# Attention steps with little filler: the value products behind the third score, the fourth score and the maxima behind them

## The chip, the cores and the metric

One Trainium2 chip, of which the program uses one core. The metric is the device time of one execution in microseconds (us); for each kernel the median of several executions is taken.

A core has several engines that run side by side, each working through its own list of instructions in order. TensorE (in the profile PE, its weight loads PEld) multiplies matrices and writes the results to PSUM, a small memory of eight banks. VectorE (DVE) and ScalarE (ACT) read PSUM and compute. GpSimd (POOL) computes on ordinary on-chip memory, and SyncE (SP) issues most of the transfers. An instruction that needs another engine's result waits on a semaphore, and everything behind it on the same engine waits too.

## The reference

Two attention layers and two gated feed-forward layers, interleaved, over 2048 tokens of width 448. The attention has 16 query heads of width 28 that share one key head and one value head. All weights are used twice, once in each layer.

```python
def _A_ref(x, wq, wk, wv, wo):            # S = 2048, D = 448, H = 16, Dh = 28
    q = (x @ wq).reshape(B, S, H, Dh).transpose(0, 2, 1, 3)
    k, v = x @ wk, x @ wv
    p = softmax(einsum("bhqd,bkd->bhqk", q, k) * Dh ** -0.5)
    o = einsum("bhqk,bkd->bhqd", p, v)
    return o.transpose(0, 2, 1, 3).reshape(B, S, H * Dh) @ wo

def _B_ref(x, w_gate, w_up, w_down):      # F = 1792
    return (sigmoid(x @ w_gate) * (x @ w_up)) @ w_down

x = x + _A_ref(layernorm(x)); x = x + _B_ref(layernorm(x))
x = x + _A_ref(layernorm(x)); x = x + _B_ref(layernorm(x))
```

## The kernel before

**Steps.** The attention of a layer is a loop of 256 steps (line 922): 16 units of queries (`u`, 128 tokens with all 16 heads each) times 16 tiles of keys (`kt`, 128 tokens each). One step does four kinds of work.

- **S, the scores** (`scores`, line 507). Four TensorE products of one key tile with four heads of the unit's queries each, 512 columns (line 510). Each goes to a PSUM bank of its own; ScalarE takes its exponential (line 513) and writes a tile `P` in ordinary memory, which sets the bank free.
- **P, the products with the values** (`pv`, line 516). They use the four tiles `P` of the step *before*, so they never wait for this step's exponentials. In the profile they are eight matmuls a step (each of the four fp32 products is run as two), and they add up in a bank of their own, not one of those that the scores use. Behind the last key tile of a unit the same function has ScalarE copy the sum out (line 525).
- **M, the maxima for the next unit** (`mx_gen`, line 464). Four more TensorE products (line 480), 512 columns each, for which VectorE takes the maximum over the keys (line 484). The scores of the next unit are shifted by these maxima. One such group of four is done per step; in two steps of a layer (`MORE`, line 902) there are two groups.
- **X, the side work** (lines 935 to 947). `tick` moves one finished unit at a time through its stages: sums, the output projection (12 matmuls, line 612), the layer norm, the split into halves, transfers. In layer 0, `paced` also lets the preparation of the weights go on, ScalarE's squares of 24 weight pieces among it (line 109).

**Filler.** Between these, at each letter F of the order, `fill.slice` (line 767) puts in matmuls of other stages, so that TensorE has work while ScalarE and VectorE drain the banks. The fillers are the query projections (`qp`, line 345 by way of `qproj`) and the feed-forward of finished blocks (`gp`, `up`, `dn`). Each matmul has a planned cost in nanoseconds (216 for one of 512 columns, 190 for one of 448, 110 for one of 256). `rate` is the planned filler of a step: what is left, divided by the steps until the next block can be fed (line 945). Each F gets a quarter of it, and what goes over is a debt on later slices. Side work, such as the output projection, counts against the same account.

**The order of a step** is one string, and the program issues the letters in this order on every engine:

```python
ORDER = "FSFSFSFSPXM"
```

So on TensorE a step is: filler, score 1, filler, score 2, filler, score 3, filler, score 4, value products, side work, maxima.

**Banks.** Scores, maxima and fillers share seven PSUM banks (line 45). A tile gets a bank that is free or next to become free in the plan of the compiler's tile layer, and its first matmul waits until the last reader of that bank is done. A query projection keeps a bank over all of its 11 matmuls, which at a low rate takes several steps; then six are left for the eight tiles of a step, four scores and four maxima.

**What is done with little filler.** At the start of a layer only the remaining query projections are there as filler, and the first feed-forward block comes in at step 49 (`FIRST`, line 903: 16 × 2 + 16 = 48 steps). From then on each block brings a planned 49,840 ns for 32 steps.

Of the kernel before, what the change touches and what calls it, by code (L numbers as in the profile page):

```python
# [19 lines left out]
def interleaved_layers_kernel(ctx: ExitStack, tc: tile.TileContext, x, wq, wk, wv, wo, wg, wu, wd, out, layers=2):  # L20
# [8 lines left out]
    F = wg.shape[1]  # L29
# [40 lines left out]
    def flush(every=False):  # L70
        todo, pend[:] = pend[:], []
        for i, (due, fn) in enumerate(todo):
            if due > now[0] and not every:
                pend.append((due, fn))
            else:
                fn()
        if every and pend:
            flush(True)
# [198 lines left out]
    def paced(step):  # L277

        k = next((i for i in range(len(PLAN) - 1) if PLAN[i + 1][0] > step), None)
        if k is None:  # L280
            n = 10 ** 6
        else:
            (a, p), (b, q) = PLAN[k], PLAN[k + 1]
            n = p + (q - p) * (step + 1 - a) / (b - a)
        while prepd[0] < n and ready[0] < 2 + FC:
            next(prep[0])
            prepd[0] += 1
# [70 lines left out]
    def layer_tiles(l):  # L358
        KK[l] = lay.tile([128, 2, S], F16, tag="KK", name="KK")
        VV[l] = lay.tile([128, KT, 32], F32, tag="VV", name="VV")  # L360
        nc.vector.memset(VV[l][:, :, 28:32], 0.0)
        nc.vector.memset(VV[l][:, :, 28:29], 1.0)
# [58 lines left out]
    def qgen(l, b):  # L421

        XT = XTQ.pop((l, b))
        for g in range(G):
            yield from qproj(l, XT, b, g)
        flush(True)
# [32 lines left out]
    def mx_ready(l, n):  # L459

        u, r = divmod(n, 4 * NB)
        return KVD[l] >= 4 * (r // 4 + 1) if u == 0 else True
# [44 lines left out]
    def scores(l, u, kt, g, P):  # L507
        assert ("m", l, u) in stored, (l, u, kt)
        s = psf.tile([128, 512], F32, tag=BANKS["s"], name="s", bufs=NBK[BANKS["s"]])
        nc.tensor.matmul(s, KK[l][0:96, 0, kt * 128:(kt + 1) * 128], QS[l, u][:, g].rearrange("p h n -> p (h n)"),  # L510
                         start=True, stop=True)
        p = wk1.tile([128, 512], F32, tag="P", name="P", bufs=8)
        nc.scalar.activation(p, s, AF.Exp, scale=esc)  # L513
        P.append(p)

    def pv(l, u, kt, P):
        if kt == 0:
            PVS[l, u] = psv.tile([128, 512], F32, tag="v", name="pv")
        v = PVS[l, u]
        for g in range(4):  # L520
            nc.tensor.matmul(v[32 * g:32 * g + 32], VV[l][:, kt], P[g], start=kt == 0, stop=kt == KT - 1,  # L521
                             tile_position=(0, 32 * g))
        if kt == KT - 1:
            o = wk1.tile([128, 512], F32, name="pvs", bufs=1)
            nc.scalar.copy(o, v)
            PVS[l, u] = o
# [5 lines left out]
    def later(*stages):  # L532

        side.append([stages[0][0], list(stages)])

    def tick():

        for s in list(side):
            s[0] -= 1
            if s[0] <= 0:  # L540
                flush()
                fill.run(s[1].pop(0)[1]())
                if s[1]:
                    s[0] = s[1][0][0]
                else:
                    side.remove(s)
# [235 lines left out]
    fill = Filler()  # L782
# [115 lines left out]
        nmx += 1  # L898

    early[0] = False  # L900
    ORDER = "FSFSFSFSPXM"
    MORE = (5, 10)
    FIRST = KT * TB + 16
    KEEP = 28000
# [1 line left out]
    for l in range(layers):  # L906
        mx = mxs[l]
        final = l + 1 == layers
        if not final:
            layer_tiles(l + 1)  # L910
        if l:
            for b in range(2, NB):
                fill.add(qgen(l, b), G * QCH)
        fill.slice(QCH)
        flush(True)
        next(mx, None)
        while late:
            late.pop(0)[1]()
        fill.slice(QCH)
        prevP = None  # L920
        rate = 0.0
        for step in range(U * KT):
            u, kt = divmod(step, KT)
            P = []
            for o in ORDER:
                if o == "S":
                    scores(l, u, kt, len(P), P)
                elif o == "M":
                    for _ in range(1 + (u == 0 and kt in MORE)):
                        next(mx, None)  # L930
                elif o == "P":
                    if prevP is not None:
                        pv(*prevP)
                elif o == "X":
                    if u and kt == 1:
                        b = (u - 1) // TB
                        if (l, b) not in BLK:
                            BLK[l, b] = Block(l, b)
                        later(*BLK[l, b].tile(u - 1))
                    if l == 0:  # L940
                        paced(step)
                    tick()
                    fed = sum(BLK[l, b].fed == TB for b in range(NBL) if (l, b) in BLK)
                    if fed < NBL - 1:
                        rate = fill.left / max(FIRST + TB * KT * fed - step, 1)
                    else:
                        rate = max(fill.left - KEEP, 0) / (U * KT - step)
                else:
                    fill.slice(rate / ORDER.count("F"))
            prevP = (l, u, kt, P)  # L950
        pv(*prevP)
        flush(True)
        later(*BLK[l, NBL - 1].tile(U - 1))
        if not final:
            mxs[l + 1] = mx_gen(l + 1)
        n = done = 0
        while (side or pend or fill.gens) if final else (side or pend or done < 4 * NB):
            tick()
            for _ in range(4):
                fill.slice(VS / 4)  # L960
            n += 1
            if not final and done < 4 * NB and QDONE.get((l + 1, 0)) == G and mx_ready(l + 1, done):
                if n >= 5 or done >= 4 * (NB - 1):
                    next(mxs[l + 1])
                    done += 1
                    n = 0
# [21 lines left out]
```

## Time and profile before

| what | value |
|---|---|
| median of 3 runs | 2358.69 us (2357.77 to 2359.82) |
| the profiled execution's own time | 2358.22 us |
| its span, first to last instruction | 2356.4 us |
| mean granted TensorE clock | 0.985 |
| TensorE busy | 2239.1 us, 95% of the span |
| VectorE busy | 1635.5 us, 69% |
| ScalarE busy | 1559.2 us, 66% |
| scores (line 510) | 2048 matmuls, 381 ns each |
| value products (line 521) | 4096 matmuls, 607 ns each, overlapping: 547.3 us together |
| maxima (line 480) | 2048 matmuls, 392 ns each, overlapping: 223.2 us together |
| exponentials (line 513) | 2048, 690 ns each |
| reductions for the maxima (line 484) | 2048, 681 ns each |

How to read it. A row of the timeline gives the start in us, the duration, the engine, the line, the operation, the tiles, and how many instructions of one kind are merged in the row. In brackets stands for how long the engine was idle before it, and which engine's instruction ended that idle time. TensorE's matmuls are pipelined and their ends are modelled, so the durations of neighbours overlap, and "busy" is no measure of what it could do: what counts is the distance from one start to the next. The share of busy time is a mean over stages that have different limits, so a change to some steps is read from those steps.

### The profile page before, as it was taken

The numbers are of one execution on the slowest core, as the hardware profiler recorded it, in microseconds if no ns is written. First come the engines' busy times: TensorE is split into PE (matmuls) and PEld (weight loads), VectorE is DVE, ScalarE is ACT, GpSimd is POOL, SyncE is SP. The second block draws the span as 40 slices with busy tenths as digits, with TensorE's granted clock in tenths as the row PEclk, the third lists the DMA queues.
The fourth block names the chain that finished last, engine by engine and source line by source line (L and its number), as shares of the span: only waits on it lengthen the run. The fifth ranks groups of instructions, "written<-read, shape, count | busy, mean of one in ns | idle before, by whom it ended". The sixth has DMA issues, their size and how long they took to land.

```text
span 2356.4 us, 41206 instructions
## 1 busy us (share of the span) xinstructions
PE 2239.1 (95%) x15736; PEld 1003.2 (43%) x15736; DVE 1635.5 (69%) x2917; ACT 1559.2 (66%) x2598; POOL 336.8 (14%) x602
## 2 busy tenths in 40 slices
PE   5888899999999999999998989999999999999999
PEld 3322243444444444444572224444444444444456
DVE  6888787777777777773358877867676777777321
ACT  5588676776667677677413777767676776767751
POOL 5203763100110110001101011000000000000010
PEclk9799999999999999999998999999999999999999
DMA  3244652323313132333342112222231313223133
GB/s 114 65 126 124 201 190 81 90 73 98 96 58 109 58 93 70 94 92 78 96 139 53 27 49 92 87 78 83 62 103 58 98 55 101 76 82 94 57 111 119
DMA packets 208071, 213.88 MB, mean 91 GB/s; under 512 B 139952, under 2 KB 168304, under 8 KB 207872
## 3 DMA queue, kind: packets, MB, share of 16 engines
q1 hardware_dynamic: 202496, 196.36, 28.5%
q0 software_dynamic: 5376, 14.87, 1.8%
q8 instruction: 123, 2.02, 0.4%
q14 instruction: 76, 0.62, 0.1%
HBM read 175.37 MB, written 23.59 MB: 84 GB/s over the span
## 4 chain that ended last, share of the span: by engine, by line
PE 51%; DVE 5%; DMA 1%; ACT 1%; issue 0%; SPq 0%; POOL 0%; ACTq 0%; DVEq 0%; POOLq 0%
PE pv L521 12%; PE s L510 10%; PE dn L702 8%; PE gp L345 7%; PE up L345 7%; DVE mp L484 4%; PE mx L480 4%; PE wo L612 2%; PE qp L345 1%; ACT P L513 0%; DMA sums<-rc 0%; DMA KK<-ktl 0%; DMA rc<-sums 0%; DMA sums<-pvs 0%; DVE st L297 0%
## 5 line engine op out<-in xcount | busy, mean ns | idle before, releaser
L513 ACT ACTIVATE P<-s,esc 128x512 f32<-128x512 f32 x2048 | 1307.8, 690 | 509.2 <-PE s L510 492.1
L484 DVE TENSOR_REDUCE mp<-mx 128x1 f32<-128x512 f32 x2048 | 1267.2, 681 | 412.2 <-PE mx L480 408.1
L510 PE MATMUL s<-QS,KK 96*128 96x512 f16 x2048 | 761.1, 381 | 52.7 <-DVE mp L484 34.8
L345 PEld LDWEIGHTS <-wgu 128*128 128x128 f16 x4928 | 458.6, 98 | 241.3 <-issue 94.5
L521 PE MATMUL pv<-P,VV 128*32 128x512 f32 x4096 | 547.3, 607 | 0.0
L345 PE MATMUL up<-XT,wgu 128*128 128x256 f16 x2464 | 375.6, 272 | 0.8 <-DVE mp L484 0.8
L345 PE MATMUL gp<-XT,wgu 128*128 128x256 f16 x2464 | 375.2, 274 | 0.2
L702 PE MATMUL dn<-WD,h 128*128 128x448 f16 x1344 | 321.7, 352 | 0.0
L510 PEld LDWEIGHTS <-KK 96*128 96x128 f16 x2048 | 194.5, 97 | 172.1 <-issue 93.0
L480 PE MATMUL mx<-KK,QH 32*128 32x512 f16 x2048 | 223.2, 392 | 20.7 <-ACT QH L402 4.8
L480 PEld LDWEIGHTS <-QH 32*128 32x128 f16 x2048 | 53.5, 91 | 396.5 <-issue 378.1
L702 PEld LDWEIGHTS <-h 128*128 128x128 f16 x1344 | 124.1, 98 | 136.6 <-issue 22.6
L521 PEld LDWEIGHTS pv<-P,VV 128*32 128x32 f32 x4096 | 80.9, 108 | 204.4 <-issue 192.6
L595 POOL TENSOR_TENSOR lb<-pvs,lb 128x512 f32<-128x512 f32 x32 | 40.5, 1265 | 800.3 <-DMA lb<-sums 679.4
L676 ACT ACTIVATE h<-th 128x512 f16<-128x512 f32 x112 | 70.2, 627 | 86.4 <-DVE th L673 86.3
L345 PE MATMUL qp<-XT,WQ 128*128 128x512 f16 x352 | 114.5, 403 | 3.8 <-DVE mp L484 2.4
L673 DVE SCALAR_TENSOR_TENSOR th<-th,up 128x512 f32<-128x512 f32 x112 | 75.8, 677 | 59.0 <-PE up L345 46.5
L303 POOL TENSOR_SCALAR rs<-mv 128x1 f32<-128x1 f32 (+2 forms) x53 | 13.6, 256 | 686.4 <-DVE mv L298 682.9
L677 DVE SCALAR_TENSOR_TENSOR h<-th,h 128x512 f16<-128x512 f32 x112 | 77.7, 693 | 46.7 <-ACT h L676 46.7
L665 ACT ACTIVATE th<-gp,gsc 128x512 f32<-128x512 f32 x112 | 76.8, 685 | 47.7 <-PE gp L345 47.7
L612 PE MATMUL wo<-WO,oT 128*128 128x448 f16 x384 | 78.4, 353 | 0.3 <-DVE oT L602 0.2
L345 PEld LDWEIGHTS <-WQ 128*128 128x128 f16 x352 | 34.2, 101 | 64.2 <-issue 41.1
(126 smaller groups left out, 834.3 us busy)
## 6 DMA issues: line engine op xcount, KB each, us to landing
wgu<-wgu_d SPq DMA_DIRECT2D x224, 512.0 KB
QS<-qd SPq DMA_DIRECT2D x384, 32.0 KB
lb<-sums SPq DMA_DIRECT2D x128, 64.0 KB
xr<-in_A_x_dram SPq DMA_DIRECT2D x32, 224.0 KB
qd<-qst POOLq DMA_DIRECT2D x28, 256.0 KB, 2.7
wgu_d<-sgu POOLq DMA_DIRECT2D x14, 512.0 KB, 3.8
QH<-qd SPq DMA_DIRECT2D x28, 128.0 KB
x2d<-x SPq DMA_DIRECT2D x16, 224.0 KB
```

What stands on the lines that cost most here:

```text
L345: nc.tensor.matmul(ps, a, b, start=n == 0, stop=n == 10)
L480: nc.tensor.matmul(ps[h], qh[32 * h:32 * h + 32, g], KK[l][32 * h:32 * h + 32, 1, kb * 512:(kb + 1) * 512], start=True, stop=True, tile_po ...
L484: nc.vector.tensor_reduce(mp[:, g, h, kb:kb + 1], ps[h], axis=AX.X, op=OP.max)
L510: nc.tensor.matmul(s, KK[l][0:96, 0, kt * 128:(kt + 1) * 128], QS[l, u][:, g].rearrange("p h n -> p (h n)"), start=True, stop=True)
L513: nc.scalar.activation(p, s, AF.Exp, scale=esc)
L521: nc.tensor.matmul(v[32 * g:32 * g + 32], VV[l][:, kt], P[g], start=kt == 0, stop=kt == KT - 1, tile_position=(0, 32 * g))
L612: nc.tensor.matmul(p, v["oT"][:, a, h * 128:(h + 1) * 128], WO[:, c, h], start=n == 0, stop=n == 11)
L665: defer(lambda: nc.scalar.activation(th, gp.rearrange("p j n -> p (j n)"), AF.Tanh, scale=gsc))
L673: nc.vector.scalar_tensor_tensor(t, th, 1.0, up.rearrange("p j n -> p (j n)"), op0=OP.add, op1=OP.mult)
L676: nc.scalar.activation(h[:, 0], t, AF.Copy, scale=2.0 ** -17)
L677: defer(lambda: nc.vector.scalar_tensor_tensor(h[:, 1], t, 2.0 ** -17, h[:, 0], op0=OP.mult, op1=OP.subtract), 1)
L702: nc.tensor.matmul(p, hs[f // 2][:, a, o:o + 128], WD[:, f, c], start=n == 0, stop=n == 3 * FC - 1)
```

## The change

```diff
@@ -898,7 +898,8 @@
     early[0] = False
-    ORDER = "FSFSFSFSPXM"
+    FULL, POOR = "FSFSFSFSPXM", "FSFSFSPFSXM"
+    ENOUGH = 800
     MORE = (5, 10)
@@ -922,7 +923,8 @@
             u, kt = divmod(step, KT)
             P = []
-            for o in ORDER:
+            order = FULL if rate > ENOUGH else POOR
+            for o in order:
                 if o == "S":
                     scores(l, u, kt, len(P), P)
@@ -946,7 +948,7 @@
                 else:
-                    fill.slice(rate / ORDER.count("F"))
+                    fill.slice(rate / order.count("F"))
             prevP = (l, u, kt, P)
```

A step whose planned filler, as the step before has left it in `rate`, is at most 800 ns takes the order `POOR`; the others keep the old one. Both strings have the same letters: four F, four S, one each of P, X and M. In `POOR` the value products stand behind the third score. The fourth slice of filler and the fourth score follow them, then the side work and the maxima. So the value products are moved past one slice of filler and one score, and nothing is added or left out.

## The prediction

> **What bounds the kernel now.** The page comes first, for the span and for where TensorE (PE) is not dense.
>
> ```profile
> span 2356.4 us, 41206 instructions
> PE 2239.1 (95%) x15736; PEld 1003.2 (43%) x15736; DVE 1635.5 (69%) x2917; ACT 1559.2 (66%) x2598; POOL 336.8 (14%) x602
> PE   5888899999999999999998989999999999999999
> DVE  6888787777777777773358877867676777777321
> ```
>
> Over most of the span PE is at 9 tenths; at the start of each layer (slices 2 to 5 and 22 to 24) it falls to 8, and there DVE rises to 8. The change acts there. The rate at step 1 is the projections left over by the 48 steps before a block is fed: stepping the planner's account of matmul costs through the program gives 417 ns in layer 0 and 297 in layer 1. It stays under 800 through step 44 of layer 0 and step 45 of layer 1; then the last leftovers are divided by two or three steps, and from step 49 a block brings over 1,500 a step. As the order goes by the rate that the step before left, 45 + 46 = 91 of the 512 steps change. The second view sums the engines over these steps, without the first of each layer, which has no value products: layer 1 (45 steps), layer 0 (steps 1 to 28, then 29 to 44), and last a stretch of dense steps.
>
> ```profile
> 1273.66:1423.84 150.18, 135.12 (x809) 33.94 (x808) 125.95 (x216) 114.05 (x190) 12.87 (x25) 1.00 0.14 41
> 102.26:200.88 98.62, 88.23 (x517) 22.69 (x516) 78.99 (x133) 89.45 (x167) 7.46 (x14) 0.98 0.42 120
> 200.88:262.32 61.44, 51.83 (x303) 13.58 (x300) 50.27 (x93) 45.10 (x75) 34.97 (x34) 0.97 0.51 154
> ...
> 1475.00:1534.00 59.00, 58.88 (x444) 28.36 (x443) 45.42 (x79) 44.33 (x71) 4.63 (x10) 1.00 0.29 87
> ```
>
> After the stretch come its length and the busy time of PE, PEld, DVE, ACT and POOL, then the granted clock. In layer 1 nothing is full: DVE is busy for 126 of 150 us, ACT for 114. In steps 1 to 28 of layer 0 ACT is busy for 89 of 98.6 us. In the dense steps PE is busy for 58.9 of 59. So layer 1 must be held by a loop of waits, which one step of the timeline shows.
>
> ```profile
> 1339.09 0.39 PE L480 MATMUL mx<-KK,QH 32*128 32x512 f16 x4
> 1339.41 0.39 PE L510 MATMUL s<-QS,KK 96*128 96x512 f16 x1
> 1339.51 2.48 DVE L484 TENSOR_REDUCE mp<-mx 128x1 f32<-128x512 f32 x4 [0.58 <-PE mx L480]
> 1339.64 0.38 PE L345 MATMUL qp<-XT,WQ 128*128 128x512 f16 x1
> 1339.86 0.77 PE L510 MATMUL s<-QS,KK 96*128 96x512 f16 x2
> 1339.90 2.42 ACT L513 ACTIVATE P<-s,esc 128x512 f32<-128x512 f32 x4 [0.71 <-PE s L510]
> 1340.85 0.38 PE L510 MATMUL s<-QS,KK 96*128 96x512 f16 x1 [0.22 <-DVE mp L484]
> 1341.16 1.06 PE L521 MATMUL pv<-P,VV 128*32 128x512 f32 x8
> 1342.15 0.39 PE L480 MATMUL mx<-KK,QH 32*128 32x512 f16 x4
> 1342.58 2.48 DVE L484 TENSOR_REDUCE mp<-mx 128x1 f32<-128x512 f32 x4 [0.58 <-PE mx L480]
> ```
>
> Count from the first reduction, at 1339.51; a reduction in the row of four takes 2.48 / 4 = 0.62. The third score is the last of its row, 0.38 before its end: 1340.25, or +0.74, 0.1 behind the end of the first reduction. The fourth waits for the second (1.24 + 0.1 = +1.34): a projection holds one of the seven banks, so the eight tiles of a step share six. Behind the fourth score stand the value products (+1.65) and the maxima (+2.64), which DVE needs 0.43 later: +3.07. DVE, idle for 0.58, starts over. The loop is second reduction, fourth score, value products, maxima, first reduction.
>
> **The change, part by part.** It removes and adds no instruction. In 89 of the 91 steps (the first step of a layer has no value products) the eight value matmuls move on PE past one score and one slice of filler; no transfer moves with them, on SP's queue or POOL's. Let T3 and T4 be the starts of the third and the fourth score. Before, the maxima start at the later of T4 and T3 + 0.22 (the spacing of two scores), plus 0.31 to the value products, plus 0.99 to the maxima. After, the value products follow the third score, so the wait of the fourth passes under them, but two more changes of operand lie on the way: score to value products, and fourth score to maxima.
>
> ```profile
> 1271.32 1.03 PE L510 MATMUL s<-QS,KK 96*128 96x512 f16 x4
> 1272.28 0.57 PE L480 MATMUL mx<-KK,QH 32*128 32x512 f16 x3
> ...
> 1354.08 1.06 PE L521 MATMUL pv<-P,VV 128*32 128x512 f32 x8
> 1355.07 2.44 PE L612 MATMUL wo<-WO,oT 128*128 128x448 f16 x12
> ```
>
> Four scores in 1.03 are (1.03 - 0.38) / 3 = 0.22 apart, so the last starts at 1271.97, and the maxima behind it at +0.31. Behind value products a full-height matmul starts after 0.99, as the maxima do. No row shows a score there; the nearest is this 0.99, and its bounds are 0.99 and 0.99 + 0.10 (the weights not hidden, below). After: T3 + 0.31 + 0.99 + 0.31 = T3 + 1.61, if no filler falls in the fourth slice. A step thus gains max(0.22, T4 - T3) - 0.31: in the step above 0.60 - 0.31 = **0.29**, leaving 2.78 and DVE still idle for 0.30. In a step without a wait it loses 0.09.
>
> The fourth slice of filler costs too. Before, its matmul lay under the wait of the fourth score; after, it stands between value products and fourth score and adds 0.22. With a wait the gain shrinks to 0.07; where the filler alone made the distance, as here (1292.27 - 1291.84 = 0.43), the step loses 0.10.
>
> ```profile
> 1291.84 0.38 PE L510 MATMUL s<-QS,KK 96*128 96x512 f16 x1 [0.24 <-ACT P L513]
> 1292.05 0.38 PE L345 MATMUL qp<-XT,WQ 128*128 128x512 f16 x1
> 1292.27 0.38 PE L510 MATMUL s<-QS,KK 96*128 96x512 f16 x1
> ...
> 1277.76 0.38 PE L510 MATMUL s<-QS,KK 96*128 96x512 f16 x1 [0.16 <-DVE mp L484]
> ...
> 1417.96 0.82 PE L510 MATMUL s<-QS,KK 96*128 96x512 f16 x2 [0.56 <-ACT P L513]
> ```
>
> Reading T4 - T3 off all 45 steps of layer 1: 24 wait without filler there (the last two rows are the fourth score of the first of these, and third and fourth of the last), 0.53 apart on average, so 24 x 0.22 = 5.3; 9 wait with filler, 0.64 apart, 9 x 0.11 = 1.0; 12 don't wait, -12 x 0.09 = -1.1. Layer 1: **5.2**. In layer 0 the same reading of steps 29 to 44 gives **1.1**, without step 40, whose fourth score waits 3.3 us on ACT in either order. The waits themselves bound this:
>
> ```profile
> DVE mp L484 <- PE mx L480: 22.6, 33, 3.2
> PE s L510 <- DVE mp L484: 7.5, 31, 0.5
> PE s L510 <- ACT P L513: 2.7, 6, 0.6
> ...
> L109 ACT ACTIVATE rmax<-rmax 128x784 f32<-128x784 f32 x24 | 22.3, 928 | 0.0
> L109 ACT ACTIVATION_READ_ACCUMULATOR rmax<-rmax 128x1 f32 x24 | 6.5, 273 | 0.0
> ...
> L402 ACT ACTIVATE qst<-qp 128x512 f16<-128x512 f32 x5 | 3.0, 610 | 0.0
> ```
>
> The first three rows are those of layer 1's stretch: PE waited for scores' banks 10.2 us (and part of each wait is hidden under the modelled end of the matmul before), DVE 22.6 us for maxima. In steps 1 to 28 of layer 0 ACT carries, beside four exponentials of 0.62 (2.48), a square of 0.93 with its read-out, on the timeline 1.07 together: 3.55, while the step is 98.62 / 28 = 3.52 long. ACT sets the pace there and an earlier maximum buys nothing; bounds 0 and 1.2 (the formula's sum), taken 0.2.
>
> Against this stands one side effect. The fourth exponential comes later: the fourth score starts at +2.04 instead of +1.34, its exponential at 2.04 + 0.43 (a score's start to its exponential, as from 1339.41 to 1339.90 with ACT free), and its bank is free at 2.47 + 0.62 + 0.1 = +3.19, which is +0.41 of the next round of 2.78. The second score of the next step needs that bank and today has no such wait; it still leaves the third at +0.74, unless filler stands in the third slice, when the third starts at 0.41 + 0.22 + 0.22 = +0.85. I price this at 0.11 in a third of the steps that gain, 33 / 3 x 0.11 = -1.2, rounded to **-1.0** as not all hit. Twice a layer, at the end of a unit, ScalarE's copy of the sum (line 525) is now issued ahead of the fourth exponential: about 0.3 late each, inside the rounding.
>
> Sum: 5.2 + 1.1 + 0.2 - 1.0 = **5.5 us** less. Behind step 49 the program order on PE is the old one and PE is dense, so what is won early is kept. The profiled execution goes from 2358.22 to 2352.7. It lies 0.47 under the median of the runs, 2358.69, so the forecast is **2353.2**.
>
> [...] Here is the row for the weights of a score, and its load is hidden: the scores above are 0.22 apart although each loads its own 128 columns in 97 ns.
>
> ```profile
> L510 PEld LDWEIGHTS <-KK 96*128 96x128 f16 x181 | 16.1, 97 | 34.3 <-issue 24.6
> ```
>
> [...]
>
> **The rivals.**
>
> 1. *The fourth exponential takes the place of the reduction* (slower). Place: the bank of the fourth score. If ACT has another 0.61 in the step (an eviction as in the L402 row), the bank is free at about +1.0, not +0.41; if that bank falls to the third score, that starts at up to +1.22, and the round is 1.22 + 1.61 + 0.43 = 3.26 instead of 3.07. It decides as soon as the bank comes later than the first reduction's, +0.74. For it: the tile layer places the banks anew, by its own plan, and six banks leave no spare. Against: ACT is free for 36 of 150 us in layer 1. With 30 steps at +0.19 and the gains gone: +5.7, **2364.4**.
> 2. *Nothing much moves*: filler drifts into the fourth slice, and gains and losses cancel. For it: 21 of 45 steps of layer 1 have filler there or no wait. Left is 1 to 3 us: **2356.7**.
> 3. *More than counted*: the new placing takes the third score's wait as well, and DVE goes back to back where it now idles 0.58. The 33 waiting steps then gain 0.58 less the filler's 0.22 in 9: 17 at most; with half of the remainder beyond the 5.5, about **2347**.
> 4. *A hidden load shows*: the load of the fourth score's weights can't pass under the value products, and each step pays its 0.10: 89 x 0.10 = 8.9 against 5.5, **2362.1**. The distance of 0.99 to the full-height matmul of line 612 speaks against it. [...]
>
> **How the numbers follow.** Chances: forecast 0.46, rival 1 0.22, rival 2 0.16, rival 3 0.10, rival 4 0.06. A measurement of this kernel can tell about 0.2% from no change: 2354.0 to 2363.4. The forecast's own spread (2350.5 to 2355.5) lies with 0.08 above the lower bound. Faster: 0.38 + 0.10 = 0.48. Rival 4 lies 1.3 under the upper bound: 0.04 of it counts as same, 0.02 as slower. Same: 0.08 + 0.16 + 0.04 = 0.28; slower: 0.22 + 0.02 = 0.24. The range of 8 in 10 takes in rivals 2, 3 and 4 and leaves out the larger part of rival 1 and the tail of 3: **2345 to 2363**.
>
> **What would show it.** Right: in layer 1 the stretch of steps 1 to 45 falls from 150.2 to about 146; PE's row of value products starts 0.31 behind the third score, the fourth score 0.99 behind it, the maxima 0.31 behind that; DVE's idle time before reductions is 0.3, not 0.58, and its sum of 22.6 falls below 19; layer 0 to step 28 stays. Wrong: scores that wait for ACT more than 2.7 us in layer 1 (rival 1), a start of over 1.05 from value products to fourth score (rival 4), or a different pace behind step 49.

## The result and the profile after

| what | before | after |
|---|---|---|
| median of 22 runs each, same chips | 2359.83 us | 2360.73 us |
| lowest to highest | 2356.7 to 2364.78 | 2356.6 to 2364.18 |
| ratio, with its 95% interval | | 1.0004 [0.9997, 1.001] |
| the profiled execution's own time | 2358.22 | 2361.08 |

The change makes no difference that can be measured. The 5.5 us less of the forecast didn't come; 2360.7 lies inside the range of 2345 to 2363. These are the lines of the page of after that answer to those of before, the span and TensorE's slices of 59 us:

```profile
span 2359.3 us, 41206 instructions
...
PE   5898899999999999999998999999999999999999
```

The picture is nearly the old one: slices 2, 4, 5 and 22 are still thin, slices 3 and 24 have gone from 8 to 9 tenths. The stretches by windows of after, layer 1 first, then steps 1 to 28 and 29 to 44 of layer 0 (columns as in the prediction):

```profile
1276.28:1426.58 150.30, 137.81 (x809) 33.10 (x808) 125.93 (x216) 117.33 (x190) 12.87 (x25) 0.99 0.14 41
102.13:202.13 100.00, 90.54 (x517) 21.87 (x516) 79.18 (x134) 90.04 (x167) 7.46 (x14) 0.98 0.42 118
202.13:264.43 62.30, 52.75 (x303) 13.07 (x299) 50.67 (x91) 46.65 (x77) 35.14 (x35) 1.00 0.50 151
```

Against before that is +0.12, +1.38 and +0.86 us, where the prediction had -5.2, -0.2 and -1.1 ahead of a side effect of +1.0. Behind step 49 nothing moved: a block of 32 steps takes 130.9 us in both. So the answer lies inside the loop, and above all in layer 1, where the expected gain was. The waits of layer 1's stretch in after:

```profile
DVE mp L484 <- PE mx L480: 21.6, 34, 3.2
...
PE s L510 <- ACT P L513: 6.1, 21, 0.9
PE s L510 <- DVE mp L484: 3.0, 10, 0.5
```

Scores wait for VectorE 3.0 us instead of 7.5, as meant, but for ScalarE 6.1 instead of 2.7 (the prediction's own sign for rival 1), and VectorE waits for maxima nearly as long as before (21.6 against 22.6). The timeline of after shows one and a half steps of it; all eight value products are merged in one row:

```profile
1336.84 0.40 PE L480 MATMUL mx<-KK,QH 32*128 32x512 f16 x4
...
1337.27 2.49 DVE L484 TENSOR_REDUCE mp<-mx 128x1 f32<-128x512 f32 x4 [0.31 <-PE mx L480]
1337.40 0.99 PE L510 MATMUL s<-QS,KK 96*128 96x512 f16 x3
...
1338.32 1.07 PE L521 MATMUL pv<-P,VV 128*32 128x512 f32 x8
...
1339.32 0.39 PE L345 MATMUL qp<-XT,WQ 128*128 128x512 f16 x1
...
1339.54 0.38 PE L510 MATMUL s<-QS,KK 96*128 96x512 f16 x1
...
1339.86 0.40 PE L480 MATMUL mx<-KK,QH 32*128 32x512 f16 x4
...
1340.02 2.43 ACT L513 ACTIVATE P<-s,esc 128x512 f32<-128x512 f32 x4 [0.30 <-PE s L510]
...
1340.76 0.38 PE L510 MATMUL s<-QS,KK 96*128 96x512 f16 x1 [0.19 <-ACT P L513]
1340.97 0.38 PE L345 MATMUL qp<-XT,WQ 128*128 128x512 f16 x1
...
1341.50 1.06 PE L521 MATMUL pv<-P,VV 128*32 128x512 f32 x8
...
1342.50 0.39 PE L510 MATMUL s<-QS,KK 96*128 96x512 f16 x1
...
1342.82 0.39 PE L480 MATMUL mx<-KK,QH 32*128 32x512 f16 x4
```

Read the starts of the maxima: 1336.84, 1339.86, 1342.82. The first round is 3.02 long: a projection stands in the fourth slice (1339.32), between value products and fourth score. The second is 2.96 long: no filler there, but the second score (1340.76) has waited for an exponential, the fourth of the step before, whose bank it takes (the row of four exponentials starts at 1340.02, and the first 0.61 of it is that one), and a projection stands behind this late score, in the third slice (1340.97). The wait alone doesn't lengthen a round. In step 31, which has no filler, the second score waits as long, and the round is 2.79:

```profile
1376.81 0.40 PE L480 MATMUL mx<-KK,QH 32*128 32x512 f16 x4
...
1377.71 0.64 PE L510 MATMUL s<-QS,KK 96*128 96x512 f16 x2 [0.18 <-ACT P L513]
...
1379.60 0.39 PE L480 MATMUL mx<-KK,QH 32*128 32x512 f16 x4
```

Before, a plain round was 3.07.

Cut in rounds from maxima to maxima, the 45 steps of layer 1 are, in us (the last column is the formula of the prediction for gains and losses, without its side effect, read off the same steps of before):

| rounds | before | after | change | formula |
|---|---|---|---|---|
| 27 plain ones | 83.8 | 81.6 | -2.3 | -4.2 |
| 4 with the doubled maxima of steps 5 and 10 in or behind them | 16.8 | 18.0 | +1.2 | -0.4 |
| 4 at a unit's turn | 12.4 | 12.7 | +0.3 | -0.9 |
| 10 with or behind the output projection | 38.1 | 38.9 | +0.8 | +0.4 |

Before, 19 of the 27 plain rounds took 3.07. After, 8 take 2.79, 7 take 2.96 or 2.97 (filler in the third slice), and 8 take 3.01 (filler in the fourth). Filler stands in the same slices before and after in all 45 steps, in 12 of them in the third and in 15 in the fourth. The +1.2 of the second group has a cause that the prediction didn't know: for 3.4 us TensorE ran at half its clock. The windows from 1290.2 on, 3.4 us each, and the timeline in the second of them:

```profile
1290.20:1293.60 3.40, 2.65 (x12) 0.69 (x12) 3.09 (x6) 1.17 (x2) 0.00 (x0) 1.00 0.00 0
1293.60:1297.00 3.40, 3.16 (x12) 0.33 (x10) 1.98 (x4) 1.49 (x3) 0.00 (x0) 0.50 0.00 0
```

```profile
1293.86 0.58 PE L510 MATMUL s<-QS,KK 96*128 96x512 f16 x1 [0.24 <-ACT P L513]
1294.37 1.94 PE L521 MATMUL pv<-P,VV 128*32 128x512 f32 x8
```

The granted clock is 0.50, a score shows 0.58 instead of 0.38, the value products 1.94 instead of 1.07. The round was 5.32 before and is 6.86 here: +1.54. Before had no such window in layer 1's stretch (clock 1.00), but one in steps 1 to 28 of layer 0 (0.51 from 171.35 to 174.75), as after has (0.51 from 139.95 to 143.35), and one in steps 29 to 44 (0.50 from 243.00 to 246.40), where after has none (1.00).

### The profile page after: what moved, and what is told of

It is laid out like the page before. It is cut to its first block, busy times and chain, and to the rows that moved or that the text cites. A ratio compares the mean times of both kernels' runs of the same rounds, so it can differ in the third digit from the quotient of the medians.

```text
span 2359.3 us, 41206 instructions
## 1 busy us (share of the span) xinstructions
PE 2245.7 (95%) x15736; PEld 1001.0 (42%) x15736; DVE 1637.0 (69%) x2917; ACT 1564.7 (66%) x2598; POOL 336.3 (14%) x602
## 4 chain that ended last, share of the span: by engine, by line
PE 52%; DVE 3%; ACT 1%; DMA 1%; issue 0%; SPq 0%; POOL 0%; ACTq 0%; DVEq 0%; POOLq 0%
PE pv L521 12%; PE s L510 11%; PE dn L702 8%; PE gp L345 7%; PE up L345 7%; PE mx L480 4%; DVE mp L484 3%; PE wo L612 2%; PE qp L345 1%; ACT P L513 1%; DMA sums<-rc 0%; DMA KK<-ktl 0%; DMA rc<-sums 0%; DMA sums<-pvs 0%; DMA XT<-hl 0%
## 5 line engine op out<-in xcount | busy, mean ns | idle before, releaser
L702 PEld LDWEIGHTS <-h 128*128 128x128 f16 x1344 | 124.1, 98 | 136.5 <-issue 22.6
```

What stands on the lines that cost most here:

```text
L702: nc.tensor.matmul(p, hs[f // 2][:, a, o:o + 128], WD[:, f, c], start=n == 0, stop=n == 3 * FC - 1)
```

## The experiments

Three theories went into the first runs. **A**: the gain of the plain rounds is real, but the wait only moved, to the exponentials and to filler that now stands between value products and fourth score. **B**: two more changes of operand in each step eat the gain. **C**: the half-clock window is what took layer 1's gain, and the new order draws it. Ratios are to the kernel before, on the same chip; each median is of 4 to 12 executions.

**The layers apart.** The new order in layer 1 alone, then in layer 0 alone.

```diff
-            order = FULL if rate > ENOUGH else POOR
+            order = FULL if rate > ENOUGH or l == 0 else POOR
```

> The new order in the poor steps of layer 1 alone; layer 0 as before. Theory A (the wait is only moved: plain steps gain 0.05 to 0.28 us each, steps in which ScalarE has anything besides its exponentials lose as much, because scores now wait for exponentials): 1 to 2 us less than before, as steps 1 to 45 of layer 1 in the profile after took 150.3 us with one window of half clock in them, worth some 1.5 us, against 150.2 before. Theory B (the two more changes of operand eat the gain in every step): 0 to 1 us more than before. Theory C (the new order draws more windows of half clock): about as after, 0.5 to 1 us more than before, and a window of half clock in the steps of layer 1.

> The new order in the poor steps of layer 0 alone. Theory A: ScalarE is the busiest there (squares and splits of the weights), so it loses: 1.5 to 3 us more than before, and TensorE waits longer for exponentials in steps 29 to 44 than the 6.1 us of before less the 3.3 of its step 40. Theory B: 0 to 1 us more, evenly over the steps. Theory C: 0 to 1 us more, and none of it left when windows of half clock are set aside.

(For layer 0 alone the condition is `l == 1`.) Measured: 2358.98 us, 0.9994 [0.9985, 1.0003], for layer 1; 2360.33, 1.0005 [0.9996, 1.0014], for layer 0. Neither can be told from no change, and neither reaches what theory A expected (1 to 2 less, 1.5 to 3 more). In the traces the layer 1 stretch is 150.35 with one half-clock window in it (the clock of the stretch is 0.99), and steps 1 to 28 of layer 0 take 100.3 and steps 29 to 44 62.0, against 98.6 and 61.4 before.

**Filler out of the fourth slice.** The third and fourth slice of filler move ahead of the second score, so no filler stands behind it.

```diff
-    FULL, POOR = "FSFSFSFSPXM", "FSFSFSPFSXM"
+    FULL, POOR = "FSFSFSFSPXM", "FSFFFSSPSXM"
```

> In the poor steps three slices of filler stand behind the first score and none behind the second and third: FSFFFSSPSXM. Filler then stands only where the second score waits for the fourth exponential of the step before anyway. Theory A: the plain steps with filler, which went from 3.07 to 2.97 and 3.0 us, go to about 2.8 as those without filler; some 30 steps of layer 1 gain another 0.1 to 0.15, and layer 0 a little: 3 to 4 us less than after, 2 to 3 less than before. Theory B: filler is not what costs, so as after within 1 us. Theory C: as after within 1 us.

Measured: 2358.11, 0.9994 [0.9985, 1.0003]. The timeline has what theory A says of the plain rounds:

```profile
1340.80 0.40 PE L480 MATMUL mx<-KK,QH 32*128 32x512 f16 x4
...
1343.59 0.40 PE L480 MATMUL mx<-KK,QH 32*128 32x512 f16 x4
...
1346.39 0.39 PE L480 MATMUL mx<-KK,QH 32*128 32x512 f16 x4
```

The rounds are 2.79 and 2.80. 11 of the 27 plain rounds take 2.79 and 7 more 2.83 or 2.84; 3.01 or 3.02 is left in two. But the stretch is 148.73, only 1.45 less than before: a stretch of half clock of 6.8 us fell into it (rounds 6 and 7, of 6.29 and 4.84, where before had 5.32 and 2.80; the clock of the stretch is 0.98, against 1.00). Where filler stands is a part of the loss.

**The price of the changes of operand.** All steps take the new order, the dense ones too, in which TensorE was busy for 58.88 of 59 us in before.

```diff
-    ENOUGH = 800
+    ENOUGH = 10 ** 9
```

> The order of the poor steps in all 512 steps. In the 421 dense steps TensorE is the bound and waits for nothing, so this measures the price of the two more changes of operand by itself. Theory A with the prediction's terms (score to value products 0.31 and fourth score to maxima 0.31 in place of 0.22 and 0.31, that is 0.09 a step): 421 x 0.09 = 38 us more than after, some 2398. With a weight load of 0.10 showing as well: 421 x 0.19 = 80 us more. Theory B needs at least 0.15 a step, since it has to eat 5.5 us in 89 steps beside the 0.09 that the prediction counted: 60 us more or above. If the dense steps hide the changes under filler: below 15 us.

Measured: 2409.38, 1.0212 [1.0198, 1.0226]; 48.7 us more than after, for 512 - 91 = 421 more steps: **0.116 per step**. A dense step of it:

```profile
1505.46 0.38 PE L510 MATMUL s<-QS,KK 96*128 96x512 f16 x1
1505.77 1.06 PE L521 MATMUL pv<-P,VV 128*32 128x512 f32 x8
...
1507.21 0.38 PE L510 MATMUL s<-QS,KK 96*128 96x512 f16 x1
1507.52 0.39 PE L480 MATMUL mx<-KK,QH 32*128 32x512 f16 x4
```

Score to value products and score to maxima are 0.31 each where matmuls of one kind stand 0.22 apart. The prediction's 0.09 was nearly right. As a theory of the whole, B falls: it needed at least 0.15 a step, and the plain rounds did fall from 3.07 to 2.79 with this price in them.

**The doubled steps in the old order, then the sum of the repairs.** First the old order in steps 5, 6, 10 and 11 of each layer; then, in layer 1 alone, that with the early filler and with the copy of the sum issued behind the fourth score.

```diff
-            order = FULL if rate > ENOUGH else POOR
+            order = FULL if rate > ENOUGH or step in (5, 6, 10, 11) else POOR
```

> After, with the old order in steps 5, 6, 10 and 11 of each layer, the two steps with a second group of maxima and those behind them. In all four profiles with the new order in layer 1 a window of half clock of 3.4 or 6.8 us begins 20 us behind that layer's first score, in step 6; in the two profiles with the old order there is none. Theory C (the window comes from the new order's work around the double maxima, and costs some 1.5 us): no such window, and 1 to 2 us less than after, level with the kernel that has the new order in layer 1 alone or better. Theory A without C (the window is chance): within 0.5 us of after, and windows there as often as not.

> Layer 0 in the old order; in layer 1 the filler ahead of the second score (FSFFFSSPSXM), the old order in steps 5, 6, 10 and 11, and ScalarE's copy of a unit's sum issued behind the fourth exponential. Theory A and C together: steps 1 to 45 of layer 1 fall from 150.2 to 145 or 146 us, the whole to 4 us less than before. Theory A alone: 2.5 us less than before. Theory B: as before within 1 us.

Measured: 2358.06, 0.9994 [0.9985, 1.0002], and 2354.52, **0.9982 [0.9973, 0.999]**. The first was to say whether the new order in those steps draws the half-clock window (C). The new order there is not needed for one: in the second kernel, which has the old order in them too, one fell into round 6 of layer 1, as in after (clock 0.53 from 1291.80 to 1295.20; the round is 6.81 us long). By the time alone C is not excluded: 0.9994 against 1.0004 for after is nearer to its 1 to 2 us less than to A's 0.5, and the intervals overlap. The second kernel also shows what the order is worth in layer 1 if the filler and the copy are put out of its way: the stretch is 147.16, 3.0 less than before, with that window in it (about 1.5 of it, an estimate from the 1.54 in after). The median is 4.9 less; what else is in that, the one profile doesn't show.

**The late copy alone**, in both layers:

```diff
-            o = wk1.tile([128, 512], F32, name="pvs", bufs=1)
-            nc.scalar.copy(o, v)
-            PVS[l, u] = o
+            def out():
+                o = wk1.tile([128, 512], F32, name="pvs", bufs=1)
+                nc.scalar.copy(o, v)
+                PVS[l, u] = o
+            outs.append(out)
...
                 elif o == "X":
+                    while outs:
+                        outs.pop()()
```

> After, with ScalarE's copy of a unit's sum issued behind the fourth exponential instead of ahead of it (it acts in four of the poor steps). Theory A: step 16 of layer 1 goes from 3.99 to 3.4 to 3.6 us and the score behind it no longer waits 0.9 us for ScalarE; the whole 0.5 to 1.5 us less than after, which the medians can hardly show. If the copy's place does not matter: step 16 stays at 3.9 or more.

Measured: 2359.3, 1.0 [0.9991, 1.0009]. At the first unit's turn of layer 1 the timeline of after has the copy and an eviction ahead of the fourth exponential:

```profile
1329.96 0.58 ACT L525 COPY pvs<-pv 128x512 f32<-128x512 f32 x1
...
1330.45 0.60 ACT L402 ACTIVATE qst<-qp 128x512 f16<-128x512 f32 x1
...
1330.93 0.69 ACT L513 ACTIVATE P<-s,esc 128x512 f32<-128x512 f32 x1
...
1331.68 0.59 PE L510 MATMUL s<-QS,KK 96*128 96x512 f16 x2 [0.91 <-ACT P L513]
```

With the late copy (its lines are shifted by one or two) the exponential comes first and the next score waits 0.45:

```profile
1328.93 0.69 ACT L514 ACTIVATE P<-s,esc 128x512 f32<-128x512 f32 x1
...
1329.51 0.58 ACT L527 COPY pvs<-pv 128x512 f32<-128x512 f32 x1
...
1329.66 0.59 PE L511 MATMUL s<-QS,KK 96*128 96x512 f16 x2 [0.45 <-ACT P L514]
```

So the copy costs 0.46 there. The other 0.45 stays, although the exponential now starts 0.42 behind its score (1328.51), as with ScalarE free; why the first score of a step waits here, and not the second, was not tested. Step 16 goes from 3.99 to 3.52, as theory A expected. The copy's cost is real, and too small to be seen in the time.

**The value products one score earlier still**, behind the second score:

```diff
-    FULL, POOR = "FSFSFSFSPXM", "FSFSFSPFSXM"
+    FULL, POOR = "FSFSFSFSPXM", "FSFSPFSFSXM"
```

> The value products one place further ahead, behind the second score (FSFSPFSFSXM). Theory A (the second score waits for the fourth exponential of the step before, so the later that score, the later the next step): third and fourth score both come behind the value products, the fourth exponential ends about 0.7 us later than after, the second score starts that much later, and a plain step is back at 3.0 to 3.1 us; 1 to 6 us more than after. Theory that only the waits for the reductions count: the value products then wait for none, a plain step takes 2.6 to 2.7 us, and it is 3 to 8 us less than after.

Measured: 2368.36, 1.0032 [1.0019, 1.0045], 7.6 us slower than after, more than theory A's 1 to 6. Layer 1's stretch is 155.12, and in its plain rounds, most of them of 3.01 to 3.23, it is again an exponential that holds the scores:

```profile
1345.88 0.38 PE L510 MATMUL s<-QS,KK 96*128 96x512 f16 x1 [0.29 <-ACT P L513]
```

The later a score comes in its step, the later its bank comes back: that is the loop of rival 1, and this run makes it the bound.

**No projection in the loop.** If the cause of the wait is the bank that a projection holds, the wait must go with it. All query projections are issued ahead of the loop, in the old order and in the new.

```diff
         while late:
             late.pop(0)[1]()
-        fill.slice(QCH)
+        fill.slice(10 ** 6)
         prevP = None
```

> Old order, with all the query projections of a layer issued ahead of its first step, so that the poor steps have no filler and all seven banks. This takes the cause of the fourth score's wait away: it then finds the bank of the first maximum, not the second. Theory A: the plain steps fall from 3.07 to between 2.5 and 2.8 us, and scores wait less for the reductions than the 7.5 us of before in layer 1; the projections cost their own time ahead of the loop instead, 52 and more of them at 0.22, so the whole ends 5 us below to 5 us above before.

> The same with the new order in the poor steps. Theory A: with seven banks there is no wait left for the value products to cover, only the 0.09 to 0.12 us of the two more changes of operand: 0 to 8 us more than with the old order and no filler. Theory that the order gains by itself, whatever the banks: 3 us or more less than with the old order and no filler.

Measured: 2364.74, 1.0023 [1.0014, 1.0032], old order, 5.4 more than before and just outside what was expected; 2368.4, 1.004 [1.0027, 1.0053], new order. The old order in the timeline of layer 1, then the new:

```profile
1350.27 0.39 PE L480 MATMUL mx<-KK,QH 32*128 32x512 f16 x4
1350.60 1.24 PE L510 MATMUL s<-QS,KK 96*128 96x512 f16 x4
...
1350.79 5.57 DVE L484 TENSOR_REDUCE mp<-mx 128x1 f32<-128x512 f32 x9
...
1352.77 0.40 PE L480 MATMUL mx<-KK,QH 32*128 32x512 f16 x4
```

```profile
1350.79 0.39 PE L480 MATMUL mx<-KK,QH 32*128 32x512 f16 x4
...
1351.21 5.01 DVE L484 TENSOR_REDUCE mp<-mx 128x1 f32<-128x512 f32 x8 [0.31 <-PE mx L480]
...
1353.32 0.39 PE L480 MATMUL mx<-KK,QH 32*128 32x512 f16 x4
```

With seven banks for the eight tiles the old order has rounds of 2.47 to 2.50 (16 of the 27 plain ones at 2.47), the fourth score waits for nothing, and VectorE goes from one row of reductions to the next without a gap. The new order takes 2.53 and leaves VectorE idle for 0.31. That it is the bank, and not the projection's own time on TensorE, shows in before: in rounds 30 to 32 a projection stood open with 2 of its 11 matmuls done, none of them was issued between one group of maxima and the next, and the round still took 3.07 (round 31):

```profile
1373.64 0.40 PE L480 MATMUL mx<-KK,QH 32*128 32x512 f16 x4
...
1376.71 0.39 PE L480 MATMUL mx<-KK,QH 32*128 32x512 f16 x4
```

So the order has no gain of its own: it goes round a shortage of one bank, and without the shortage it costs 0.06 a step.

**The projections ahead in layer 1 alone**, in the old order: in layer 0 of the run above the loop began 18.5 us later than before, and step 49 still came 12.0 later.

```diff
-        fill.slice(QCH)
+        fill.slice(10 ** 6 if l else QCH)
```

> The old order throughout; in layer 1 alone the remaining query projections are issued ahead of the first step, so that its poor steps have seven banks and no filler. In the runs without filler the plain steps of layer 1 took 2.47 us against 3.07, and the stretch from the first score of layer 1 to the first block's matmul 147.5 us against 162.4; layer 0, where ScalarE sets the pace, got nothing back for the 18.5 us that its loop began later. Theory A (banks held by the projection are the cause of the wait): the projections cost some 14 us ahead of the loop, the steps give back more: 10 to 17 us less than before. If the stretch only moved its time to the head of the layer: within 2 us of before.

Measured: 2352.4, **0.9971 [0.9959, 0.9982]**: the fastest of all, 6.9 us under the kernel before, though less than expected. Steps 0 to 49 of layer 1, before and here, from windows:

```profile
1271.27:1437.97 166.70, 151.24 (x913) 39.81 (x912) 138.99 (x237) 127.23 (x212) 15.73 (x29) 1.00 0.14 41
```

```profile
1284.97:1429.31 144.34, 134.44 (x828) 32.31 (x827) 133.38 (x229) 122.44 (x206) 10.87 (x23) 0.99 0.11 30
```

The loop starts 13.7 us later and its first 50 steps take 22.4 less, so step 50 comes 8.7 earlier; the next 32 steps take 133.5 instead of 130.9, and from there on both are alike. What is left is 6.0 by the trace, about the 6.9 measured.

## Where the prediction was right and where it was wrong, point by point

- **What bounds layer 1: right.** The loop of second reduction, fourth score, value products and maxima, closed by the shortage of a bank, was the bound. The pair without projections shows it: without the shortage a plain round takes 2.47, and in the rows above no score waits.
- **The distances of the new order: right.** Third score to value products 0.31, value products to fourth score 0.99 to 1.00, fourth score to maxima 0.32, and the undisturbed round 2.79 where 2.78 was forecast, with VectorE idle for 0.31. Rival 4 is refuted: its load would have made 1.09 of the 0.99 to 1.00 from value products to fourth score.
- **"24 x 0.22 = 5.3", "9 x 0.11", "-12 x 0.09": right as far as they go.** The filler stayed in its slices, and 25 of the 45 rounds of layer 1 changed by what the formula gives, to 0.05.
- **"Against this stands one side effect", -1.0: this step failed.** It was far too small: the rounds of layer 1 fall 5.3 short of the formula, 3.8 of it without the half-clock window. The fourth exponential is late, and so is what ScalarE has to do around it; the prediction followed only one of these waits, and that at too low a price. Three parts:
  - "0.11 in a third of the steps". The case is the one described, filler in the third slice behind a late second score, but it costs 0.18 (2.97 - 2.79). The distance from a score's start to its exponential was taken as 0.43; the rows named for it, 1339.41 and 1339.90, are 0.49 apart. With 0.49 the bank is free at +0.47 and the third score starts at +0.91, 0.17 behind +0.74. It hit 7 plain rounds, not 11, so this part came to 1.3 in place of 1.2; that the sum is nearly right is luck.
  - "About 0.3 late each, inside the rounding", for the copy at a unit's turn. At the first turn the next score waited 0.91, 0.46 of it for the copy, and rounds 17 and 33 fell 0.83 and 0.41 short of the formula: 1.2 together, of which the late copy took back 0.8.
  - Not priced: 0.3 in step 13, whose round is 3.58 in both kernels because the transpose ahead of its maxima (line 499) waits for VectorE in both; 0.3 in step 38, whose first score waits 0.45 for ScalarE; 0.5 in the ten rounds of the output projection. What is left of the 3.8 comes in amounts of 0.1 and less.
- **Layer 0, steps 1 to 28, "ACT sets the pace there", "bounds 0 and 1.2": wrong.** The 3.55 adds up durations. On the timeline of before, rows of four exponentials start at 103.55 and 106.66 with one square and its read-out between them: ScalarE comes round in 3.11, while steps 1 to 3 take 3.34 to 3.55. The changes of rounds 1 to 8 follow the formula to 0.02, losses and gains alike. Rounds 10, 12, 13, 23 and 24, with filler in the third slice, fall 0.25 to 0.36 short of it, and the two at a unit's turn 0.2 each. Each kernel has one half-clock window here (the clock of the stretch is 0.98 in both), and these cancel. The sum is +1.38.
- **Layer 0, steps 29 to 44, "1.1": wrong.** 0.86 more came. Step 40, in which before had a half-clock window, is 2.1 shorter, so the other 15 steps lost 3.0. Steps 34, 36, 38 and 43 lose 0.45 to 0.71 each. In step 34 the third score waits for the first exponential of its own step, in both kernels; before, then after:

```profile
217.55 0.73 ACT L130 ACTIVATE sgu<-rgu,swb 128x512 f16<-128x512 f32 x1
...
219.06 0.38 PE L510 MATMUL s<-QS,KK 96*128 96x512 f16 x1 [0.40 <-ACT P L513]
```

```profile
218.97 0.69 ACT L513 ACTIVATE P<-s,esc 128x512 f32<-128x512 f32 x1 [0.44 <-PE s L510]
219.56 0.71 ACT L130 ACTIVATE sgu<-rgu,swb 128x512 f16<-128x512 f32 x1
220.17 1.83 ACT L513 ACTIVATE P<-s,esc 128x512 f32<-128x512 f32 x3
...
220.90 0.38 PE L510 MATMUL s<-QS,KK 96*128 96x512 f16 x1 [0.72 <-ACT P L513]
```

  In after ScalarE idles 0.44 for the late fourth score; only behind its exponential come the 0.71 for the weights of the next stage and the first exponential of the step, so the wait grows from 0.40 to 0.72. In steps 38 and 43 ScalarE idles 0.44 and 0.57 in the same place. This is close to rival 1 ("another 0.61 in the step"), though the third score waits for the exponential of its own step, not for the fourth of the step before.
- **Half-clock windows: not in the prediction.** The one in layer 1 of after cost 1.54 (a round of 6.86 in place of 5.32), as much as fifteen plain rounds of 2.97 win over 3.07. Where they fall differs from profile to profile: layer 1's stretch has a clock of 1.00 in before and 0.99 in after, steps 29 to 44 of layer 0 one of 0.97 and 1.00.

The mechanism is that of rival 1: the wait for a reduction became a wait for an exponential. Its price was smaller than rival 1's 5.7, so the outcome lies between rival 2 and rival 1; the filler that drifts, which rival 2 named, was not seen. That 2360.7 lies in the range is no success of the sum, whose 2353.2 missed by 7.5: the range was drawn wide enough for the rivals. Without the window layer 1 won 1.4 us (0.12 - 1.54). Layer 0 lost 1.4 and 0.9, or up to 2.4 in the latter if the window that before had there cost 1.5 too. The sum, 0.9 to 2.4 more, is compatible with the measured -0.7 to +2.4, which also takes in no change.

## What to carry to other kernels

When an order is changed under a shortage of buffers, follow each buffer to its next user: the instruction that is moved back gives its own buffer back later, and the wait comes again at whoever takes it (in layer 1 scores waited 4.5 us less for VectorE and 3.4 more for ScalarE). Follow also what else the engine of the late instruction has to do around it: here a copy and pieces of weights, priced at nothing, cost about as much as the one wait that was priced. And a shortage is better removed than gone round: issuing the holder of the seventh bank ahead of the loop took 22 us out of 50 steps and cost 14 ahead of them and 3 behind, where the new order, the half-clock window set aside, took 1.4 out of 45.

## What the runs showed of the hardware that was not expected

The half-clock windows of after did not follow a long idle time. In the first of the rows from 1290.20 above TensorE had no gap longer than 0.30 us, and yet the next 3.4 us ran at 0.50; in the 3.4 us ahead of the window at 139.95 the longest gap is 0.29. In before the longest gap ahead of the window at 171.35 is 1.04, and the one at 243.00 lies at the end of a gap of 3.31. Both windows of after fall behind doubled maxima, in the rounds whose maxima start at 136.53 and 1290.29. In the latter 4.4 us pass without a value product, from 1289.97 to 1294.37. But before has 4.3 at the same place in layer 1, from 1288.25 to 1292.58, and its clock stays at 1.00 there.

Whether the new order draws more of these windows (theory C) stays open. With filler in the loop, the clock of layer 1's stretch is 0.98 or 0.99 in five profiles with one of the new orders there (after, the layer 1 alone, the early filler, the sum of the repairs, the value products behind the second score) and 1.00 in the two with the old order (before and the layer 0 alone). But without filler it is 0.99 in the two with the old order and 1.00 in the one with the new. Each kernel has a single profile, so this proves little. What brings a window on was not tested, nor whether the windows make the spread of single runs; among those of after the fastest, 2356.6, has a mean clock of 0.988 and the slowest, 2364.18, one of 0.985.
